# A Fourier mix and a three-way maxout layer on one Trainium2 core: TensorE's order written in the source, the input turned on GpSimd, the fold's output laid out by component, and the opening reordered

## The chip, the cores and the metric

The kernel runs on one core of one Trainium2 chip. The metric is device time in microseconds: the median of several executions. TensorE multiplies (PE in the profile; PEld is its weight load), VectorE is DVE, ScalarE is ACT, GpSimd is POOL, and SP issues the DMAs that store the output. Inputs and outputs are float32 in device memory; the matmuls take bfloat16.

## The reference, cut to what matters

```
def _attn_ref(x):                      # x: (8, 3072, 256)
    X = np.fft.fft(x, axis=1)
    X = np.fft.fft(X, axis=2)
    return X.real
def _moe_ref(x, w1, w2, w3, w_out):    # x: (24576, 256), d_ff = 768
    h = np.maximum(np.maximum(x @ w1, x @ w2), x @ w3)
    return h @ w_out
out = _moe_ref(x=_attn_ref(x).reshape(24576, 256), ...)
```

## The kernel before, in words

The work is done batch by batch (8 batches of 3072 tokens by 256 features). The transform along the sequence is split as 3072 = 24 x 128. The transform along the features is never done by itself: its matrix is multiplied into the weights once, in `prep_first` (gE, gO, gD) and `prep_second` (gw, gwr), so that a batch needs three steps only.

**Step 1, `fnet`, lines 265 to 341.** The input of a batch lies in `x0` as 96 partitions (4 feature groups of 24 rows) by 128 positions by 64 features. For each of the 64 features a matmul of 96 columns (L270) has a 96 x 128 slice of `x0` as its weights and the small matrix `m24blk` as its moving operand. The slice takes every 64th element, so its columns lie 128 bytes apart. Five features fill one PSUM tile `ps`, and ACT copies it into `ub` (L272); the list `DLS` has 13 such groups. DVE then folds feature f with feature 256 - f into sums `zE` and differences `zO` (L280): four operations of 600 elements, eight of 240 and eight of 216, and a few small ones (L289 to L297). `zE` and `zO` have the feature outside and the 24 or 26 components inside. The second stage multiplies by cosine and sine tables, 50 matmuls of up to 128 columns (L318 to L326, and three of one column in L332 to L334); their weights are columns of `zE` or `zO` that lie 48 or 52 bytes apart. ACT writes the result to `tE` and `tO` (L329), and POOL makes reversed copies `tEr` and `tOr` (L339, L340).

**Step 2, units.** A batch has 3 blocks of 512 columns, and a block has 6 units, one for each 128 of the 768 hidden features. In a unit `unit_plus` (L349, L350) runs four matmuls of 512 columns: two into the PSUM tile `pse2` and two into `pse3`. `unit_out` lets ACT write the relu of `pse2` to `stmp` (L363) and DVE take the maximum of `pse3` and `stmp` into `hp` (L364). Then `unit_minus` (L357) adds one more matmul into each of the same two tiles, which makes them the mirrored columns, and `unit_out` runs again, into `hm`. So the added matmul may not start before `hp` has been read out of its tile. Each of `pse2`, `pse3` and `stmp` has two buffers.

**Step 3, the output, `l2_block`.** For each 128 columns of a block 16 matmuls of 256 columns go into a PSUM tile `po` (L367, L369, L372); DVE copies it to `ot` (L392), and SP stores it (L399). These run from a queue, 11 matmuls after each unit, and the rest at the end of a block. A last short piece for one middle row of each batch is `l2_mid`: six little units of 8 columns and 8 matmuls.

**What sets the order.** The source is written in one order, but a scheduler moves the instructions of each engine. Only POOL has its order by hand, in the opening: the 16 DMAs of `x0` for batch 0, with two iotas (`kidx` and `dvec`, L128 and L130) between the fourth and the fifth, then the weights, then `x0` for batch 1. In the opening DVE makes the index tables from `kidx` (L176 to L182), ACT takes their sine into `cos_t` and `sin_t` (L183), and `md` follows from `dvec` (L195 to L205). Engines run their own instructions strictly in order.

Of the kernel before, what the change touches and what calls it, by code (L numbers as in the profile page):

```python
# [9 lines left out]
FP32 = mybir.dt.float32  # L10
# [24 lines left out]
def kernel(  # L35
# [28 lines left out]

    consts = ctx.enter_context(tc.tile_pool(name="consts", bufs=1))
    ps_f = ctx.enter_context(tc.tile_pool(name="ps_f", bufs=2, space=bass.MemoryType.PSUM))
    ps_l1 = ctx.enter_context(tc.tile_pool(name="ps_l1", bufs=2, space=bass.MemoryType.PSUM))
    ps_o = ctx.enter_context(tc.tile_pool(name="ps_o", bufs=2, space=bass.MemoryType.PSUM))
    x0_pool = ctx.enter_context(tc.tile_pool(name="x0", bufs=2))
# [14 lines left out]
    v2_bf = consts.tile([128, 2 * DFF], BF16, tag="v2_bf")  # L84
    v3_bf = consts.tile([128, 2 * DFF], BF16, tag="v3_bf")
# [11 lines left out]
    def load_x0(b, between):  # L97
        x0 = x0_pool.tile([96, 128 * 64], BF16, name="x0", tag="x0")
        xr = x[b].rearrange("(a bb) (g dl) -> g a bb dl", bb=128, g=4)
        x0v = x0.rearrange("p (bb dl) -> p bb dl", dl=64)  # L100
        for ch in range(4):
            if ch in between:
                between[ch]()
            for g in range(4):
                nc.gpsimd.dma_start(  # L105
                    out=x0v[g * 24:(g + 1) * 24, ch * 32:(ch + 1) * 32, :],
                    in_=xr[g, :, ch * 32:(ch + 1) * 32, :])
        return x0
# [17 lines left out]
    def between():  # L126

        nc.gpsimd.iota(kidx, [[1, 13], [24, 128]], base=0, channel_multiplier=0,  # L128
                       allow_small_or_imprecise_dtypes=True)
        nc.gpsimd.iota(dvec, [[1, 64], [64, 2]], base=0, channel_multiplier=0,  # L130
                       allow_small_or_imprecise_dtypes=True)

    with tc.manual_schedule(engines={mybir.EngineType.Pool}):
        x0_tiles = {0: load_x0(0, {1: between})}

# [8 lines left out]
        x0_tiles[1] = load_x0(1, {})  # L144
# [28 lines left out]
    for (dst, shift) in ((cos_t, 768.0), (sin_t, 0.0)):  # L173
        v = gen.tile([128, 13 * 128], FP32, name="v", tag="v", bufs=2)
        q = gen.tile([128, 13 * 128], FP32, name="q", tag="q", bufs=2)
# [14 lines left out]
    for fc in range(2):  # L190
# [10 lines left out]
        vi = gen.tile([128, 256], INT32, name="vi", tag="vi", bufs=2)  # L201
# [14 lines left out]
    for zO in zO_tiles:  # L216
        nc.vector.memset(zO.rearrange("p (c r) -> p c r", r=26)[:, :, 24:26], 0.0)
        nc.vector.memset(zO[:, 0:26], 0.0)

    def prep_first():  # L220

        for jh in range(2):
            cs = slice(jh * 384, (jh + 1) * 384)
            for i, (wv, vv) in enumerate(((w2_bf, v2_bf), (w3_bf, v3_bf))):
                w3d, v3d, w13d = (t.rearrange("p (fc j) -> p fc j", fc=2)[:, :, cs]
                                  for t in (wv, vv, w1_bf))
                tc.keep_in_program_order(
                    nc.vector.tensor_tensor(out=v3d, in0=w3d, in1=w13d, op=ALU.subtract))
                for (half, dst) in ((0, gE[i]), (1, gO[i])):
                    psg = ps_f.tile([128, 512], FP32, name="psg", tag="ps")  # L230
                    for fc in range(2):
# [5 lines left out]
                nc.vector.tensor_scalar(out=gD[i][:, cs], in0=gO[i][:, cs], scalar1=dif,  # L237
                                        scalar2=None, op0=ALU.mult)

    def prep_second():  # L240

        for jp in range(NJC // 2):
# [8 lines left out]
            nc.scalar.copy(out=g1t[:, jp * 512:(jp + 1) * 512], in_=pst)  # L251
        psw = ps_f.tile([128, 512], FP32, name="psw", tag="ps")
        for half in range(2):
            for jc in range(NJC):
# [7 lines left out]
                                op0=ALU.mult)  # L262

    def fnet(b, x0):
        x0r = x0.rearrange("p (bb dl) -> p bb dl", dl=64)
        ub = u_pool.tile([128, 64 * 96], BF16, name="ub", tag="ub")
        for (d0, d1) in DLS:
            ps1 = ps_f.tile([128, 512], FP32, name="ps1", tag="ps")
            for i in range(d1 - d0):
                nc.tensor.matmul(ps1[:, i * 96:(i + 1) * 96], x0r[:, :, d0 + i], m24blk,  # L270
                                 start=True, stop=True)
            nc.scalar.copy(out=ub[:, d0 * 96:d1 * 96], in_=ps1[:, 0:(d1 - d0) * 96])  # L272

# [3 lines left out]
        e = zE.rearrange("p (dl g r) -> p dl g r", g=2, r=24)  # L277
        o = zO.rearrange("p (dl g r) -> p dl g r", g=2, r=26)
        def fold(dst, op, lo, hi, g):
            nc.vector.tensor_tensor(out=dst[:, lo:hi, g, 0:24], in0=u[:, lo:hi, g, :],  # L280
                                    in1=u[:, 64 - lo:64 - hi:-1, 3 - g, :], op=op)

        for ranges in (((20, 45),), ((10, 20), (45, 55)), ((1, 10), (55, 64))):
            for (dst, op) in ((e, ALU.add), (o, ALU.subtract)):
                for (lo, hi) in ranges:
                    for g in range(2):
                        fold(dst, op, lo, hi, g)
                if ranges[0][0] == 1:
                    nc.vector.tensor_tensor(out=dst[:, 0, 1, 0:24], in0=u[:, 0, 1, :],  # L289
                                            in1=u[:, 0, 3, :], op=op)  # L290
                    if dst is e:
                        nc.vector.tensor_copy(e[:, 0, 0, :], u[:, 0, 0, :])

        nc.vector.tensor_scalar(out=o[:, 0, 0, 1:12], in0=u[:, 0, 2, 13:24], scalar1=-1.0,
                                scalar2=None, op0=ALU.mult)
# [130 lines left out]
    for b in range(B):  # L426
        tt = fnet(b, x0_tiles.pop(b))
        if b == 0:
            prep_first()
# [60 lines left out]
```

## Time and profile before

| | us |
|---|---|
| median of 3 runs (lowest to highest) | 500.73 (500.02 to 501.63) |
| the profiled execution's own time | 499.23 |
| its span, from the first to the last instruction | 497.1 |
| PE busy / DVE busy / ACT busy / POOL busy | 453.5 / 320.4 / 260.9 / 140.6 |
| first matmul starts | 27.46 |
| first matmul of the second stage of batch 0 starts | 37.30 |
| first matmul of step 3 starts | 63.69 |

The times in all views count from the start of the span. A matmul's shown duration includes the time in which it drains, so the rate of PE is read from the distance of starts, not from durations. Rows of a view group instructions by line and shape; the mean of one is in ns, and idle time before them stands behind the bar.

### The profile page before, as it was taken

The numbers are of one execution on the slowest core, as the hardware profiler recorded it, in microseconds if no ns is written. First come the engines' busy times: TensorE is split into PE (matmuls) and PEld (weight loads), VectorE is DVE, ScalarE is ACT, GpSimd is POOL, SyncE is SP. The second block draws the span as 40 slices with busy tenths as digits, with TensorE's granted clock in tenths as the row PEclk, the third lists the DMA queues.
The fourth block names the chain that finished last, engine by engine and source line by source line (L and its number), as shares of the span: only waits on it lengthen the run. The fifth ranks groups of instructions, "written<-read, shape, count | busy, mean of one in ns | idle before, by whom it ended". The sixth has DMA issues, their size and how long they took to land.

```text
span 497.1 us, 9195 instructions
## 1 busy us (share of the span) xinstructions
PE 453.5 (91%) x3408; PEld 315.6 (63%) x3408; DVE 320.4 (64%) x662; ACT 260.9 (52%) x472; POOL 140.6 (28%) x160
## 2 busy tenths in 40 slices
PE   0056999999999999999999999999999999999995
PEld 0055447785568657785669666875669566866664
DVE  8834674657676576657666567657675666667663
ACT  1355652575436653575446644665457644765440
POOL 9979800029000750029000840048000100020000
PEclk9999899999999999999999999999999999999998
DMA  8999992219921692219911793119911022102122
GB/s 48 75 164 99 98 32 86 84 44 108 105 86 66 59 133 99 73 44 109 126 65 65 74 123 102 65 46 120 134 64 65 22 65 84 65 22 65 65 84 86
DMA packets 163436, 40.05 MB, mean 81 GB/s; under 512 B 136512, under 2 KB 163392, under 8 KB 163392
## 3 DMA queue, kind: packets, MB, share of 16 engines
q0 software_dynamic: 135536, 14.30, 70.6%
q1 hardware_dynamic: 27856, 25.18, 16.1%
q8 instruction: 26, 0.43, 0.4%
q14 instruction: 18, 0.15, 0.1%
HBM read 28.31 MB, written 25.17 MB: 108 GB/s over the span
## 4 chain that ended last, share of the span: by engine, by line
PE 78%; DVE 3%; ACT 2%; POOL 2%; DMA 1%; issue 1%; DVEq 0%; ACTq 0%
PE po L372 23%; PE pse L349 12%; PE pse L357 11%; PE pse L350 11%; PE ps L270 8%; PE po L367 4%; PE po L369 4%; POOL x L105 2%; PE ps L318 2%; DMA x<-in_x_dram 1%; PE ps L324 1%; PE ps L326 1%; ACT stmp L363 1%; PE ps L321 1%; DVE zE L280 1%
## 5 line engine op out<-in xcount | busy, mean ns | idle before, releaser
L363 ACT ACTIVATE stmp<-pse 128x512 bf16<-128x512 f32 (+1 forms) x294 | 167.7, 588 | 164.3 <-PE pse L350 128.6
L364 DVE TENSOR_TENSOR hp<-pse,stmp 128x512 bf16<-128x512 f32 x144 | 99.1, 690 | 99.1 <-PE pse L357 39.8
L105 POOL DMA_DIRECT2D x<-in_x_dram x128 | 109.5, 863 | 8.1 <-DMA x<-in_x_dram 3.6
L349 PE MATMUL pse<-tE,gE 128*128 128x512 bf16 x288 | 108.8, 379 | 1.7 <-DVE hm L364 0.7
L350 PE MATMUL pse<-tO,gO 128*128 128x512 bf16 x288 | 109.1, 380 | 0.0
L364 DVE TENSOR_TENSOR hm<-pse,stmp 128x512 bf16<-128x512 f32 x144 | 99.0, 687 | 11.8 <-ACT stmp L363 9.3
L357 PE MATMUL pse<-tO,gD 128*128 128x512 bf16 x288 | 94.8, 380 | 1.1 <-ACT stmp L363 0.6
L339 POOL COPY tEr<-tE 128x1536 bf16<-128x1536 bf16 x8 | 11.8, 1471 | 289.1 <-ACT tE L329 289.1
L372 PE MATMUL po<-wout_bf,hp 128*128 128x256 bf16 x576 | 92.6, 272 | 0.0
L372 PE MATMUL po<-wout_bf,hm 128*128 128x256 bf16 x576 | 89.1, 272 | 0.1
L270 PE MATMUL ps<-m24blk,x 96*128 96x96 bf16 x512 | 57.4, 250 | 28.8 <-DMA w_bf<-in_moe_w_dram 27.5
L270 PEld LDWEIGHTS <-x 96*128 96x128 bf16 x512 | 55.9, 199 | 33.1 <-DMA w_bf<-in_moe_w_dram 27.4
L392 DVE COPY ot<-po 128x512 f32<-128x512 f32 x96 | 65.5, 684 | 14.5 <-PE po L372 13.8
L372 PEld LDWEIGHTS <-hm 128*128 128x128 bf16 x576 | 56.1, 99 | 17.3 <-DVE hm L364 0.4
L372 PEld LDWEIGHTS <-hp 128*128 128x128 bf16 x576 | 56.2, 100 | 14.2
L272 ACT CAST ub<-ps 128x480 bf16<-128x480 f32 (+1 forms) x104 | 55.4, 554 | 15.6 <-PE ps L270 13.3
L357 PEld LDWEIGHTS <-gD 128*128 128x128 bf16 x288 | 28.1, 98 | 29.8 <-issue 1.5
L350 PEld LDWEIGHTS <-gO 128*128 128x128 bf16 x300 | 29.4, 98 | 27.1 <-issue 12.2
L349 PEld LDWEIGHTS <-gE 128*128 128x128 bf16 x300 | 29.5, 99 | 21.1 <-issue 2.6
L280 DVE TENSOR_TENSOR zE<-ub 128x240 bf16<-128x240 bf16 (+2 forms) x80 | 20.2, 311 | 33.9 <-ACT ub L272 33.9
L367 PE MATMUL po<-gw,tE 128*128 128x256 bf16 x96 | 26.2, 272 | 0.0
L369 PE MATMUL po<-gwr,tOr 128*128 128x256 bf16 x96 | 26.2, 272 | 0.0
(99 smaller groups left out, 359.5 us busy)
## 6 DMA issues: line engine op xcount, KB each, us to landing
out_dram<-ot SPq DMA_DIRECT2D x176, 128.0 KB, 1.7
x<-in_x_dram POOLq DMA_DIRECT2D x128, 96.0 KB, 6.7
out_dram<-ot SPq DMA_DIRECT2D x24, 64.0 KB, 6.7
w_bf<-in_moe_w_dram POOLq DMA_DIRECT2D x6, 192.0 KB, 6.2
out_dram<-ot SPq DMA_DIRECT2D x8, 63.0 KB
wout_bf<-in_moe_w_out_dram POOLq DMA_DIRECT2D x1, 384.0 KB, 8.6
out_dram<-ot SPq DMA_DIRECT2D x1, 8.0 KB
```

Source lines behind the costliest of these rows:

```text
L105: nc.gpsimd.dma_start(out=x0v[g * 24:(g + 1) * 24, ch * 32:(ch + 1) * 32, :], in_=xr[g, :, ch * 32:(ch + 1) * 32, :])
L270: nc.tensor.matmul(ps1[:, i * 96:(i + 1) * 96], x0r[:, :, d0 + i], m24blk, start=True, stop=True)
L272: nc.scalar.copy(out=ub[:, d0 * 96:d1 * 96], in_=ps1[:, 0:(d1 - d0) * 96])
L349: nc.tensor.matmul(pse[:, 0:n], gE[i][:, js], te, start=True, stop=False)
L350: nc.tensor.matmul(pse[:, 0:n], gO[i][:, js], to, start=False, stop=True)
L357: nc.tensor.matmul(pse, gD[i][:, js], to, start=False, stop=True, skip_group_check=True)
L363: nc.scalar.activation(out=stmp[:, 0:n], in_=pses[0][:, 0:n], func=AX.Relu)
L364: nc.vector.tensor_tensor(out=dst, in0=src3, in1=stmp[:, 0:n], op=ALU.max)
L367: nc.tensor.matmul(po, te, gw[:, 0:256], start=True, stop=False)
L369: nc.tensor.matmul(po, to, wo, start=False, stop=False)
L372: nc.tensor.matmul(po, hcols(jc), wout_bf[:, jc * 256:(jc + 1) * 256], start=False, stop=(jc == NJC - 1))
L392: nc.vector.tensor_copy(out=ot, in_=po)
```

## The change

It has five parts.

1. **PE's and POOL's order is the source's.** The whole main loop stands under a manual schedule for these two engines. Unit u now runs: the added matmul of unit u-1 into `pse2`, the two matmuls into a new `pse2`, the added matmul of unit u-1 into `pse3`, the two into a new `pse3` (L379 to L386). Then come five matmuls of step 3, one step of `fnet` for the next batch, and the other five or six of step 3. `fnet` is now a generator with a step per group of five features or per PSUM tile of the second stage, and a table tells which unit takes which step: units 0 to 12 the 13 groups, units 14 to 17 the second stage. The folds are written right behind groups 4, 8 and 12. DVE and ACT keep the scheduler.
2. **The input is turned on POOL.** From batch 1 on, the DMAs land in four buffers `xs`, and four `tensor_copy` on POOL (L113), 96 partitions by 2048 elements each, write them to `x0` with the 128 positions of one feature side by side. The weights of the first stage (now L298) then have contiguous columns. Batch 0 is still read with a step of 128 bytes.
3. **`zE` and `zO` have the component outside and the feature inside.** The second stage's weights (now L342 to L350) become contiguous. The fold (now L290) runs over features in its inner loop: it writes neighbours and reads `ub` with a step of 192 bytes. It has the same elements as before.
4. **The opening.** All 16 DMAs of batch 0 come ahead of the two iotas. The index table of the sine is made in place in `kidx`, with one buffer each for `v`, `q` and `vi`. Every second PSUM tile of batch 0's first stage is copied by DVE (L301), not by ACT. `prep_first` stands as one piece ahead of the first unit, and takes its differences in place.
5. **The middle row** is two pieces of one PSUM tile each, in units 8 and 10 of the last batch, with one relu and one maximum for all six little units.

The diff, cut to its core:

```
+    FOLDS = {4: ((20, 45),), 8: ((10, 20), (45, 55)), 12: ((1, 10), (55, 64))}
...
+    def fetch_chunk(b, ch):
+        xs = xs_pool.tile([96, 32 * 64], BF16, name="xs", tag="xs")
+        load_chunk(b, ch, xs)
+        return xs
+
+    def turn_chunk(xs, x0, ch):
+
+        nc.gpsimd.tensor_copy(
+            x0.rearrange("p (dl bb) -> p dl bb", bb=128)[:, :, ch * 32:(ch + 1) * 32],
+            xs.rearrange("p (bb dl) -> p dl bb", dl=64))
...
+    with tc.manual_schedule(engines={mybir.EngineType.Pool}):
+        x0_tiles = {0: new_x0(), 1: new_x0()}
+        for ch in range(4):
+            load_chunk(0, ch, x0_tiles[0][:, ch * 2048:(ch + 1) * 2048])
         nc.gpsimd.iota(kidx, [[1, 13], [24, 128]], base=0, channel_multiplier=0,
                        allow_small_or_imprecise_dtypes=True)
...
-        x0_tiles[1] = load_x0(1, {})
+        second = [fetch_chunk(1, ch) for ch in range(4)]
...
         def fold(dst, op, lo, hi, g):
-            nc.vector.tensor_tensor(out=dst[:, lo:hi, g, 0:24], in0=u[:, lo:hi, g, :],
-                                    in1=u[:, 64 - lo:64 - hi:-1, 3 - g, :], op=op)
+            nc.vector.tensor_tensor(
+                out=dst[:, lo:hi, g, 0:24].rearrange("p dl r -> p r dl"),
+                in0=u[:, lo:hi, g, :].rearrange("p dl r -> p r dl"),
+                in1=u[:, 64 - lo:64 - hi:-1, 3 - g, :].rearrange("p dl r -> p r dl"), op=op)
...
+            if b == 0 and i % 2:
+                nc.vector.tensor_copy(ub[:, d0 * 96:d1 * 96], ps1[:, 0:(d1 - d0) * 96])
+            else:
+                nc.scalar.copy(out=ub[:, d0 * 96:d1 * 96], in_=ps1[:, 0:(d1 - d0) * 96])
+            if i in FOLDS:
...
+            yield
...
+    def unit_mm(te, to, jc, last):
...
+        for i in range(2):
+            if last is not None:
+                minus_mm(last, i)
+            pse = ps_l1.tile([128, TOKB], FP32, name=f"pse{i + 2}", tag=f"pse{i + 2}")
+            nc.tensor.matmul(pse, gE[i][:, js], te, start=True, stop=False)
+            nc.tensor.matmul(pse, gO[i][:, js], to, start=False, stop=True)
+            pses.append(pse)
...
+    with tc.manual_schedule(engines={mybir.EngineType.PE, mybir.EngineType.Pool}):
+        tts = {0: []}
+        run(fnet(0, x0_tiles.pop(0), tts[0]), 19)
+        prep_first()
+        for ch in range(4):
+            turn_chunk(second[ch], x0_tiles[1], ch)
...
+                plan = ({6: 2, 7: 2, 8: 2, 9: 2, 10: 2, 11: 2, 12: 1} if b == 0 else
+                        {u: 1 for u in range(13)})
+                plan.update({14: 1, 15: 2, 16: 2, 17: 1})
...
+                n = 11 if jc < 4 else 10
+                l2_some(n // 2)
+                run(steps, plan.get(u, 0))
+                run(extra, int(1 <= u <= 4))
+                l2_some(n - n // 2)
...
+                    if u == 0:
+                        x0_tiles[b + 2] = new_x0()
+                        fetched = [fetch_chunk(b + 2, 0), fetch_chunk(b + 2, 1)]
+                    if u in (4, 8):
+                        turn_chunk(fetched[u // 4 - 1], x0_tiles[b + 2], u // 4 - 1)
+                        fetched.append(fetch_chunk(b + 2, u // 4 + 1))
+                    if u in (11, 14):
+                        turn_chunk(fetched[u // 4], x0_tiles[b + 2], u // 4)
```

How instructions stand now, at three places. First PE in the middle of a batch, one unit, each matmul behind its weight load; before (`gD0` and `gD1` are the weights of the added matmuls; the number behind `pse2` and `pse3` tells the unit's tile):

```order
L349 LDWEIGHTS gE0_98
L349 MATMUL pse2_2055<-tE_1796,gE0_98 128x512
L350 LDWEIGHTS gO0_100
L350 MATMUL pse2_2055<-tO_1797,gO0_100 128x512
L357 LDWEIGHTS gD0_102
L357 MATMUL pse2_2007<-tO_1797,gD0_102 128x512
L349 LDWEIGHTS gE1_99
L349 MATMUL pse3_2056<-tE_1796,gE1_99 128x512
L350 LDWEIGHTS gO1_101
L350 MATMUL pse3_2056<-tO_1797,gO1_101 128x512
L357 LDWEIGHTS gD1_103
L357 MATMUL pse3_2008<-tO_1797,gD1_103 128x512
```

And the same place of the changed kernel:

```order
L386 LDWEIGHTS gD0_103
L386 MATMUL pse2_1939<-tO_1724,gD0_103 128x512
L379 LDWEIGHTS gE0_99
L379 MATMUL pse2_1976<-tE_1723,gE0_99 128x512
L380 LDWEIGHTS gO0_101
L380 MATMUL pse2_1976<-tO_1724,gO0_101 128x512
L386 LDWEIGHTS gD1_104
L386 MATMUL pse3_1943<-tO_1724,gD1_104 128x512
L379 LDWEIGHTS gE1_100
L379 MATMUL pse3_1980<-tE_1723,gE1_100 128x512
L380 LDWEIGHTS gO1_102
L380 MATMUL pse3_1980<-tO_1724,gO1_102 128x512
```

The added matmul into `pse3` of the unit before has moved from the end of the unit to its fourth place, and every unit now has this same order.

Second DVE at the folds in the middle of the run; before:

```order
L364 TENSOR_TENSOR hp<-pse_2367,stmp 128x512
L364 TENSOR_TENSOR hm<-pse_2337,stmp 128x512
L392 COPY ot<-po 128x512
L364 TENSOR_TENSOR hm<-pse_2367,stmp 128x512
L280 TENSOR_TENSOR zE<-ub 128x25x24 x2
L280 TENSOR_TENSOR zO_248<-ub 128x25x24 x2
L392 COPY ot<-po 128x512
L280 TENSOR_TENSOR zE<-ub 128x10x24 x4
L280 TENSOR_TENSOR zO_248<-ub 128x10x24 x4
L280 TENSOR_TENSOR zE<-ub 128x9x24 x4
```

And in the changed kernel, around the first and the second part of the folds:

```order
L393 TENSOR_TENSOR hp<-pse_2777,stmp 128x512
L421 COPY ot<-po 128x512
L290 TENSOR_TENSOR zE<-ub 128x24x25 x2
L290 TENSOR_TENSOR zO_252<-ub 128x24x25 x2
L393 TENSOR_TENSOR hm<-pse_2777,stmp 128x512
```

```order
L393 TENSOR_TENSOR hp<-pse_2932,stmp 128x512
L290 TENSOR_TENSOR zE<-ub 128x24x10 x4
L290 TENSOR_TENSOR zO_252<-ub 128x24x10 x4
L421 COPY ot<-po 128x512
L393 TENSOR_TENSOR hm<-pse_2932,stmp 128x512
L393 TENSOR_TENSOR hp<-pse_2983,stmp 128x512
```

The folds stood behind the last maximum of a batch, with only copies of `ot` between them; now they stand between the `hp` and the `hm` of one unit, and the next unit's `hp` is behind them.

Third DVE in the opening, from the end of the index tables to the first folds of batch 0; before:

```order
L202 CAST vi<-vm 128x256
L205 CAST vm<-vi 128x256
L185 TENSOR_SCALAR nsin_t<-sin_t 128x1664
L203 TENSOR_SCALAR vi<-vi 128x256
L205 CAST vm<-vi 128x256
L280 TENSOR_TENSOR zE<-ub 128x25x24 x2
L280 TENSOR_TENSOR zO_248<-ub 128x25x24 x2
L280 TENSOR_TENSOR zE<-ub 128x10x24 x4
```

And now:

```order
L190 TENSOR_TENSOR kidx<-kidx,q 128x1664
L213 CAST vm<-vi 128x256
L205 TENSOR_SCALAR vm<-dvec,pf 128x128
L301 CAST ub<-ps_266 128x480
L207 TENSOR_SCALAR vm<-pf 128x1
L301 CAST ub<-ps_280 128x480
L193 TENSOR_SCALAR nsin_t<-sin_t 128x1664
L210 CAST vi<-vm 128x256
L301 CAST ub<-ps_298 128x480
L211 TENSOR_SCALAR vi<-vi 128x256
L290 TENSOR_TENSOR zE<-ub 128x24x25
```

DVE's copies of the first stage's PSUM tiles (L301) stand behind the whole chain on `kidx`, and between the rest of the tables and the folds.

## What the change does to the time, predicted blind

> **What bounds the kernel now.** I read the page first, for the share of each engine and the chain that ended last.
>
> ```profile
> span 497.1 us, 9195 instructions
> PE 453.5 (91%) x3408; PEld 315.6 (63%) x3408; DVE 320.4 (64%) x662; ACT 260.9 (52%) x472; POOL 140.6 (28%) x160
> PE 78%; DVE 3%; ACT 2%; POOL 2%; DMA 1%; issue 1%; DVEq 0%; ACTq 0%
> ```
>
> PE is busy for 91% of the span and carries 78% of the last chain. Its idle time is nearly all in the first 37 us. Second, the windows between the POOL copies `tEr` of batches 1 to 7, six whole batches (length, then busy time of PE, PEld, DVE, ACT and POOL, the granted clock, the share of the DMA engines).
>
> ```profile
> 107.86:164.21 56.35, 55.45 (x422) 38.61 (x421) 36.32 (x74) 30.80 (x57) 15.77 (x18) 1.00 0.91 86
> ...
> sum 331.25, PE 329.16 PEld 230.71 DVE 218.64 ACT 186.43 POOL 81.78; mean PE 54.86 PEld 38.45 DVE 36.44 ACT 31.07 POOL 13.63
> ```
>
> A batch takes 331.25 / 6 = 55.2 us, PE works in nearly all of it at full clock, and DVE in 36.4. So a batch costs what PE's stream costs, and that is read from distances of starts in PE's timeline.
>
> ```profile
> 69.52 0.38 PE L350 MATMUL pse<-tO,gO 128*128 128x512 bf16 x1
> 69.74 0.38 PE L357 MATMUL pse<-tO,gD 128*128 128x512 bf16 x1
> ...
> 100.32 0.58 PE L270 MATMUL ps<-m24blk,x 96*128 96x96 bf16 x5
> 100.74 0.27 PE L372 MATMUL po<-wout_bf,hm 128*128 128x256 bf16 x1
> 100.85 0.27 PE L367 MATMUL po<-gw,tE 128*128 128x256 bf16 x1
> ...
> 105.23 0.23 PE L318 MATMUL ps<-cos_t,zE 128*128 128x128 bf16 x1
> 105.30 0.23 PE L321 MATMUL ps<-sin_t,zE 128*128 128x128 bf16 x1
> ```
>
> 512 columns take 0.216 us, 256 take 0.109, five of the first stage 0.42, and 128 columns of the second stage 0.07. Per batch that is 108 x 0.216 = 23.3, 192 x 0.109 = 20.9, 13 x 0.42 = 5.4 and 50 x 0.07 = 3.5: 53.1 us. The other 2.1 us of the 55.2 are waits.
>
> **Contiguous weights.** By the columns that are multiplied, five matmuls of 96 would take 5 x 96/256 x 0.109 = 0.20 us and not 0.42, and 128 columns 0.055 and not 0.07. What differs is the weight load.
>
> ```profile
> L270 PEld LDWEIGHTS <-x 96*128 96x128 bf16 x512 | 55.9, 199 | 33.1 <-DMA w_bf<-in_moe_w_dram 27.4
> L318 PEld LDWEIGHTS <-zE 128*128 128x128 bf16 x104 | 14.6, 162 | 4.8 <-DVE zE L292 4.7
> L372 PEld LDWEIGHTS <-hm 128*128 128x128 bf16 x576 | 56.1, 99 | 17.3 <-DVE hm L364 0.4
> ...
> 483.08 0.17 PE L349 MATMUL pse<-t_mid,gE 128*128 128x8 bf16 x1
> 483.10 0.17 PE L350 MATMUL pse<-t_mid,gO 128*128 128x8 bf16 x1
> ```
>
> A load with a step of 128 bytes takes 199 ns, one of 48 bytes 162, a contiguous one 99. Behind contiguous loads two matmuls of 8 columns start 0.02 us apart, so such a load does not pace anything as wide as 96. I take the column rate: 13 x 0.215 = 2.8 and 50 x 0.055 = 2.7, against 5.4 and 3.5. That is 3.4 us a batch, for seven batches (batch 0 is still read with the step): **-23.8**. If a load paced at its 99 ns, five would take 0.50 and nothing would come of it; the 0.02 excludes that.
>
> **Waits that go.** From the first matmul of step 3 to the end:
>
> ```profile
> 63.69 0.27 PE L367 MATMUL po<-gw,tE 128*128 128x256 bf16 x1
> ...
> 491.45 0.69 DVE L392 COPY ot<-po 128x512 f32<-128x512 f32 x1 [1.05 <-PE po L372]
> ```
>
> are 433.4 us. Work in them: 828 x 0.216 = 178.8 (864 less the first six units), 1536 x 0.109 = 167.4, 7 x 8.9 = 62.3 for the transforms, 3 for the middle row, and 5.7 from 491.4 to the end of the span: 417.2. So 16.2 us are waits: the first block without step 3 beside it, the scheduler's ends of batches, and the middle row's six turns between PE, ACT and DVE. The new order gives each unit of a later block its ten or eleven matmuls of step 3 as cover, so **-16.2**, and +3 for small ones that stay. The middle row in two pieces does 1.5 us less: **-1.5**.
>
> **What the folds cost in their new place.** Here the change gives back. The rows:
>
> ```profile
> L364 DVE TENSOR_TENSOR hp<-pse,stmp 128x512 bf16<-128x512 f32 x144 | 99.1, 690 | 99.1 <-PE pse L357 39.8 <-ACT stmp L363 32.2 <-PE pse L350 26.7
> L392 DVE COPY ot<-po 128x512 f32<-128x512 f32 x96 | 65.5, 684 | 14.5 <-PE po L372 13.8
> ...
> L363 ACT ACTIVATE stmp<-pse 128x512 bf16<-128x512 f32 x288 | 166.6, 597 | 161.6 <-PE pse L350 126.3 <-DVE hp L364 11.4 <-PE pse L357 7.7
> L272 ACT CAST ub<-ps 128x480 bf16<-128x480 f32 x96 | 52.0, 560 | 15.6 <-PE ps L270 13.3
> L280 DVE TENSOR_TENSOR zE<-ub 128x240 bf16<-128x240 bf16 x32 | 6.9, 277 | 2.7 <-ACT ub L272 2.7
> L280 DVE TENSOR_TENSOR zE<-ub 128x600 bf16<-128x600 bf16 x16 | 6.8, 468 | 24.5 <-ACT ub L272 24.5
> L182 DVE TENSOR_TENSOR v<-v,q 128x1664 f32<-128x1664 f32 x2 | 3.7, 1882 | 0.0
> ...
> 50.80 1.29 DVE L364 TENSOR_TENSOR hp<-pse,stmp 128x512 bf16<-128x512 f32 x2
> ```
>
> Two maxima in a row take 1.29, so each costs the queue about 0.61, as does an `ot`. The folds today, on packed bf16, gain an element in (468 - 277) / 360 = 0.53 ns. The two other shapes of the same operation, L364 and L182, need (1882 - 690) / 1152 = 1.03 ns. No row has a fold that reads with a step. Bounds: 0.53 if the step costs nothing, 1.03 and above if it takes the packing away. I take 1.03, since its reads are no longer neighbours; 600 elements are then 0.77 us alone and about 0.70 behind one another, 240 about 0.33, 216 about 0.30. The three bursts are 4 x 0.70 = 2.8, 8 x 0.33 = 2.6 and 8 x 0.30 with six small ones 2.9 us, against 1.6, 1.6 and 2.1 by the lower bound.
>
> The Trainium skill (VectorE: DVE Perf Modes, Mode 2×_1P) asks 16-bit data with a step of one for two elements a cycle, which speaks against this change and for my choice; the 0.53 and the 1.03 are such a pair.
>
> Now one unit, from its start, PE's drain of 0.17 and 0.05 for a wait included. The added matmul into `pse3` ends at 0.86, so `hm` of the unit before runs on DVE from 1.1 and `hp` from 1.7 to 2.4, `ot` to 3.0 where there is one. The group's last matmul ends at 2.1, and ACT's copy to `ub` at 2.9. So the burst begins at 2.9, not earlier. Queued behind it on DVE are `ot` (0.61, not in every unit), the next `hm` (0.61) and `hp` (0.69). PE needs that `hp` at its fourth place two units on, 5.2 to 5.5 + 0.65 = 5.85 to 6.1. First burst: 2.9 + 2.8 + 0.61 + 0.69 + 0.05 = 7.05 against 5.85. Second, with `ot` ahead: 2.9 + 2.6 + 0.61 + 0.61 + 0.69 + 0.05 = 7.46 against 6.1. Third, whose next unit is shorter: 2.9 + 2.9 + 0.61 + 0.61 + 0.69 + 0.05 = 7.76, less about 0.6 where no `ot` falls there, against 5.87. PE stands at the added matmul, with the next two into `pse3` and all of the unit's step 3 queued behind it, for 1.2, 1.4 and 1.3 us, 3.9 a batch: **+27.3** for seven batches. In the kernel before the folds had a stretch of step 3 alone as cover; at the lower bound they wait 0, 0.3 and 0.5 us, +5.6 in all.
>
> **The turn on POOL.**
>
> ```profile
> L339 POOL COPY tEr<-tE 128x1536 bf16<-128x1536 bf16 x8 | 11.8, 1471 | 289.1 <-ACT tE L329 289.1
> ...
> 44.73 3.21 DVE L237 TENSOR_SCALAR gD<-gO,dif 128x384 bf16<-128x384 bf16 x1 [6.00 <-ACT gO L236]
> ...
> 44.94 1.48 POOL L339 COPY tEr<-tE 128x1536 bf16<-128x1536 bf16 x1
> 46.35 1.47 POOL L340 COPY tOr<-tO 128x1536 bf16<-128x1536 bf16 x1
> ```
>
> At this rate 2048 elements are 1.96 us; with reads in steps twice that, 3.9, is the other bound, as with the folds. I take 2.9. Four are 11.6 us a batch beside the 13.6 that POOL works now, and it has 50, and the turn is a batch ahead of its use, so its own time is hidden, and so is its wait for the landing of its four DMAs, behind which the next four issues are queued. For batch 1 it has from about 51, behind `tOr` of batch 0, to 63 us, and PE asks at about 67. The Trainium skill (GPSIMD Engine Reference, Performance pitfalls for Q7 kernels) puts a read whose step is above 8 bytes at half as much again; by that the copy would be an estimated 2.9 us.
>
> But a DVE operation of 384 elements took 3.21 us while these two copies ran, to 47.94, when the second ended: they hold something that DVE needs. A fold that meets a turn would wait for its end. After the 8 DMAs at a batch's start the turns lie near 9, 15, 21 and 25 us, the bursts near 14, 26 and 37; I take a quarter of a turn a batch, 0.7 us, six batches: **+4**.
>
> **The opening.**
>
> ```profile
> 4.89 1.62 POOL L128 IOTA kidx<- 128x1664 f32 x1
> 6.43 0.86 POOL L130 IOTA dvec<- 128x128 f32 x1
> ...
> 8.88 6.57 POOL L105 DMA_DIRECT2D x<-in_x_dram  x1
> ...
> 31.65 0.81 POOL L105 DMA_DIRECT2D x<-in_x_dram  x1 [0.16 <-issue]
> ...
> 9.23 2.07 DVE L176 TENSOR_SCALAR v<-kidx,pidx 128x1664 f32<-128x1664 f32 x2
> 11.23 1.95 DVE L178 TENSOR_SCALAR q<-v 128x1664 f32<-128x1664 f32 x2
> ...
> 27.46 1.09 PE L270 MATMUL ps<-m24blk,x 96*128 96x96 bf16 x10 [27.46 <-DMA w_bf<-in_moe_w_dram]
> ...
> 37.30 0.33 PE L318 MATMUL ps<-cos_t,zE 128*128 128x128 bf16 x1 [1.66 <-DVE zE L292]
> 48.46 0.81 PE L232 MATMUL psg<-v_bf,md 128*128 128x384 bf16 x4 [3.05 <-DVE v_bf L228]
> ```
>
> One DMA's issue stood for 6.57 us while DVE ran the tables; with the iotas behind it this goes, and the input lands about 7 us earlier, near 20 (5.8 of the stall and 2.5 of the iotas, less about 1 as the DMA engines fill). But the tables now start behind 16 issues of 0.81 and both iotas, at 17, not 9.2. Their chain is about 12.4 us, to 29.5 (2.1, twice 1.95 and 3.7 for the eight large ones, 2.7 for the small ones now among them), and DVE's six copies of the first stage stand behind it, with `nsin_t`, the rest of the tables and three bursts: 14 us and 1 of waits. So `zE` is ready near 43 and `zO` near 44.6, not 37.3. Second stage 4 us, `prep_first` 5.5 without the wait of 3.05, six units 36 x 0.216 with the second preparation's 24 matmuls and 1 of waits 11.4: step 3 begins near 65.7, against 63.69: **+2**, between -2 and +8.
>
> **The sum.** 497.1 - 23.8 - 16.2 + 3 - 1.5 + 27.3 + 4 + 2 = 491.9 of span. The profiled execution took 499.23, 2.1 more than its span, so 494.0; the median of the runs is 1.5 above that one, so I forecast **495.5**, 1.0% faster.
>
> **Rivals.** *The folds stay cheap or covered* (faster): at the lower bound 27.3 becomes 5.6, and 474. For it: DVE has 55.2 - 36.4 = 19 us a batch free; against it: the queue behind the burst, and a read without neighbours. Chance 0.18. *Turn and fold collide* (the slower one): DVE stood behind two POOL copies in the row of L237. If a fold does so too, and POOL gets its turn in between two folds of a burst, a whole turn falls into the first and into the second burst. Two of 2.9 us are 5.8 a batch, PE waits as long since the bursts have used up its slack, 6 x 5.8 - 4 = +31, so 526; half of that is 511. It decides from about one whole turn a batch. The Trainium skill (SBUF — State Buffer, Who interferes with whom) has a DVE instruction with two SBUF inputs wait for a GpSimd instruction that reads SBUF, which would be every fold beside a turn; no run so far shows one. L237 speaks for it; the 6.57 us speak against, since there POOL got no gap between DVE's operations. Chance 0.25. *The load is not what paces the small matmuls*, so the contiguous layout does nothing: +23.8, 519; the 0.02 us speaks against. Chance 0.04. My forecast has 0.53, by itself 485 to 505 (the opening's bounds, and bursts of 2 to 4.5 us a batch).
>
> **How the numbers follow.** About 0.3% is what a measurement of this kernel can tell from no change: 499.2 to 502.2. Of the forecast's 0.53 about 0.39 lies below, 0.09 within and 0.05 above; the first rival is faster, the two others slower, but for 0.03 of the collision that ends within. Faster 0.57, same 0.12, slower 0.31. The range of 8 in 10 takes in the first rival and most of the second: 474 to 513.
>
> **What would show it.** Right: first-stage loads near 99 ns from batch 1 on and a group of five in 0.22; folds of 600 near 0.77 us; three waits of about 1.3 us a batch on PE, at the added matmul, released by DVE `hp`; a batch of 54 to 55 us; second stage of batch 0 at 43 to 45. Wrong: folds near 0.47 us or no wait behind them (faster), folds of 3 us beside a turn, or a first-stage matmul of batch 1 that waits for POOL (slower).

## Result: a quarter slower, and the profile after

The changed kernel takes 623.51 us (median of 4 runs, 620.46 to 627.04) against 500.38 before: ratio 1.2463, 95% interval 1.2388 to 1.2539. The forecast was 495.5, with 474 to 513 as its range. The profiled run took 622.65, its span is 620.9.

The page of the changed kernel, span, engines and the clock of its 40 slices:

```profile
span 620.9 us, 9266 instructions
PE 432.1 (70%) x3356; PEld 297.2 (48%) x3408; DVE 461.3 (74%) x663; ACT 250.8 (40%) x461; POOL 243.2 (39%) x188
PEclk9999966898698976999679895899958999999999
```

PE has less work than before (432 against 454 us; the records of 52 of its 3408 matmuls are missing) and stands for 30% of the span; DVE has 141 us more. The windows between the `tEr` copies show where (columns as before: length, busy PE, PEld, DVE, ACT, POOL, clock):

```profile
126.63:202.19 75.56, 53.42 (x411) 36.46 (x417) 57.64 (x74) 30.44 (x56) 31.14 (x22) 0.86 0.49 64
...
501.73:559.14 57.41, 49.92 (x412) 34.77 (x418) 42.68 (x74) 30.49 (x57) 2.92 (x2) 1.00 0.17 56
```

Six batches last from 48.95 to 501.73, 75.5 us each. The last one before the end, in which POOL has nothing to fetch or turn, takes 57.4. Both are longer than the 55.2 before. 6 x 18.1 = 108 us belong to the batches with turns.

The groups by form, busy time and mean ns behind the bar:

```profile
L290 DVE TENSOR_TENSOR zE<-ub 128x600 bf16<-128x600 bf16 x16 | 82.7, 5206 | 0.4 <-ACT ub L303 0.4
L290 DVE TENSOR_TENSOR zO<-ub 128x600 bf16<-128x600 bf16 x16 | 44.3, 2811 | 0.0
L290 DVE TENSOR_TENSOR zE<-ub 128x240 bf16<-128x240 bf16 x32 | 16.1, 566 | 3.1 <-ACT ub L303 3.1
L298 PEld LDWEIGHTS <-x 96*128 96x128 bf16 x512 | 36.9, 114 | 34.1 <-DMA w_bf<-in_moe_w_dram 20.8
L386 PE MATMUL pse<-tO,gD 128*128 128x512 bf16 x288 | 111.3, 387 | 140.8 <-DVE hp L393 140.1
L113 POOL COPY x<-xs 96x2048 bf16<-96x2048 bf16 x28 | 107.3, 3848 | 6.8 <-DMA xs<-in_x_dram 5.4
```

The weight loads fell to 114 ns as expected (batch 0 still has its step). The second stage's matmuls start 0.055 to 0.06 us apart, as expected too; that of batch 0 begins at 43.1, inside the 43 to 45 that were named. Step 3 begins at 68.43 (63.69 before), from PE's timeline:

```profile
68.43 0.27 PE L396 MATMUL po<-gw,tE 128*128 128x256 bf16 x1
...
551.07 0.22 PE L342 MATMUL ps<-cos_t,zE 128*128 128x128 bf16 x1
551.13 0.22 PE L345 MATMUL ps<-sin_t,zE 128*128 128x128 bf16 x1
```

But a fold of 600 into `zE` takes 5.2 us as the mean and one into `zO` 2.8, where 0.77 was forecast, and PE stands 140 us at the added matmul, behind `hp`. POOL's and DVE's timelines around one first burst:

```profile
138.07 3.75 POOL L113 COPY x<-xs 96x2048 bf16<-96x2048 bf16 x1 [0.86 <-DMA xs<-in_x_dram]
141.77 3.22 POOL L102 DMA_DIRECT2D xs<-in_x_dram  x4
144.98 3.63 POOL L113 COPY x<-xs 96x2048 bf16<-96x2048 bf16 x1
148.55 3.23 POOL L102 DMA_DIRECT2D xs<-in_x_dram  x4
151.78 8.13 POOL L113 COPY x<-xs 96x2048 bf16<-96x2048 bf16 x2
```

```profile
139.03 0.68 DVE L393 TENSOR_TENSOR hp<-pse,stmp 128x512 bf16<-128x512 f32 x1
...
142.94 13.48 DVE L290 TENSOR_TENSOR zE<-ub 128x600 bf16<-128x600 bf16 x2
156.34 5.68 DVE L290 TENSOR_TENSOR zO<-ub 128x600 bf16<-128x600 bf16 x2
161.94 0.68 DVE L393 TENSOR_TENSOR hm<-pse,stmp 128x512 bf16<-128x512 f32 x1
```

Four folds last 19.0 us, from 142.94 to 161.94. The two on `zE` end at 149.7 and 156.4, each 1.0 to 1.1 us after a turn (148.6 and 155.4): a fold ran when a turn was done, and the next turn got in before the next fold. A maximum `hp` beside a turn (139.03), which reads PSUM and one SBUF tensor, takes its usual 0.68. In the batch without turns the same burst is this:

```profile
518.03 2.28 DVE L290 TENSOR_TENSOR zE<-ub 128x600 bf16<-128x600 bf16 x2
520.22 2.25 DVE L290 TENSOR_TENSOR zO<-ub 128x600 bf16<-128x600 bf16 x2
522.36 0.70 DVE L393 TENSOR_TENSOR hm<-pse,stmp 128x512 bf16<-128x512 f32 x1
```

4.33 us. So a first burst with turns is 14.7 us longer, the time in which PE does nothing grows by as much (from 7.5 to 22.1 us), and its busy time rises from 49.9 to 53.4 us at a clock of 0.86: 14.7 + 3.5 = 18.2 of the 18.1 us.

### The profile page after: what moved, and what is told of

Read it like the earlier page. It is cut to its first block, busy times and chain, and to the rows that moved or that the text cites. A ratio compares the mean times of both kernels' runs of the same rounds, so it can differ in the third digit from the quotient of the medians.

```text
span 620.9 us, 9266 instructions
## 1 busy us (share of the span) xinstructions
PE 432.1 (70%) x3356; PEld 297.2 (48%) x3408; DVE 461.3 (74%) x663; ACT 250.8 (40%) x461; POOL 243.2 (39%) x188
## 4 chain that ended last, share of the span: by engine, by line
PE 58%; DVE 29%; issue 7%; POOL 2%; ACT 2%; DMA 0%; DVEq 0%; SPq 0%; POOLq 0%
PE po L401 17%; DVE zO L290 11%; PE pse L380 10%; PE pse L386 10%; DVE zE L290 9%; PE pse L379 7%; PE po L396 3%; PE po L398 3%; PE ps L298 3%; DVE hp L393 2%; DVE hm L393 2%; POOL x L102 2%; PE ps L348 1%; DVE ot L421 1%; PE ps L350 1%
## 5 line engine op out<-in xcount | busy, mean ns | idle before, releaser
L392 ACT ACTIVATE stmp<-pse 128x512 bf16<-128x512 f32 x288 | 158.9, 595 | 204.6 <-DVE hm L393 149.2
L386 PE MATMUL pse<-tO,gD 128*128 128x512 bf16 x288 | 111.3, 387 | 140.8 <-DVE hp L393 140.1
L290 DVE TENSOR_TENSOR zE<-ub 128x240 bf16<-128x240 bf16 (+2 forms) x80 | 113.5, 1477 | 6.5 <-ACT ub L303 6.5
L113 POOL COPY x<-xs 96x2048 bf16<-96x2048 bf16 x28 | 107.3, 3848 | 6.8 <-DMA xs<-in_x_dram 5.4
L379 PEld LDWEIGHTS <-gE 128*128 128x128 bf16 x288 | 28.4, 99 | 164.3 <-issue 148.7
L401 PE MATMUL po<-wout_bf,hm 128*128 128x256 bf16 x576 | 95.5, 278 | 0.1
L102 POOL DMA_DIRECT2D xs<-in_x_dram x112 | 91.9, 828 | 2.3 <-DMA xs<-in_x_dram 1.3
L379 PE MATMUL pse<-tE,gE 128*128 128x512 bf16 x238 | 92.5, 389 | 0.0
L421 DVE COPY ot<-po 128x512 f32<-128x512 f32 x96 | 65.9, 686 | 21.7 <-PE po L401 21.4
L290 DVE TENSOR_TENSOR zO<-ub 128x240 bf16<-128x240 bf16 (+2 forms) x80 | 74.8, 994 | 0.0
L298 PE MATMUL ps<-m24blk,x 96*128 96x96 bf16 x512 | 42.2, 221 | 30.7 <-DMA w_bf<-in_moe_w_dram 20.8
L401 PEld LDWEIGHTS <-hm 128*128 128x128 bf16 x576 | 55.2, 100 | 17.2 <-issue 1.1
L298 PEld LDWEIGHTS <-x 96*128 96x128 bf16 x512 | 36.9, 114 | 34.1 <-DMA w_bf<-in_moe_w_dram 20.8
L386 PEld LDWEIGHTS <-gD 128*128 128x128 bf16 x288 | 28.4, 99 | 19.1 <-issue 0.3
```

The lines of the kernel that those rows point to most:

```text
L102: nc.gpsimd.dma_start(out=dst[g * 24:(g + 1) * 24, :].rearrange("p (bb dl) -> p bb dl", dl=64), in_=xr[g, :, ch * 32:(ch + 1) * 32, :])
L113: nc.gpsimd.tensor_copy(x0.rearrange("p (dl bb) -> p dl bb", bb=128)[:, :, ch * 32:(ch + 1) * 32], xs.rearrange("p (bb dl) -> p dl bb", dl ...
L290: nc.vector.tensor_tensor(out=dst[:, lo:hi, g, 0:24].rearrange("p dl r -> p r dl"), in0=u[:, lo:hi, g, :].rearrange("p dl r -> p r dl"), i ...
L298: nc.tensor.matmul(ps1[:, k * 96:(k + 1) * 96], x0r[:, d0 + k, :], m24blk, start=True, stop=True)
L379: nc.tensor.matmul(pse, gE[i][:, js], te, start=True, stop=False)
L386: nc.tensor.matmul(pses[i], gD[i][:, jc * 128:(jc + 1) * 128], to, start=False, stop=True, skip_group_check=True)
```

## The experiments

**Theory A**: a fold, which has two SBUF inputs, stands while POOL reads SBUF in a turn; the turns are the damage and the scattered folds' own length a smaller one. **Rival B**: the scattered access itself makes the folds that slow, with or without turns. Ratios are to the kernel before, with 95% intervals.

**No turn.** Every batch is loaded as batch 0 is, so the first stage's weights have their step again.

```diff
-        second = [fetch_chunk(1, ch) for ch in range(4)]
+        for ch in range(4):
+            load_chunk(1, ch, x0_tiles[1][:, ch * 2048:(ch + 1) * 2048])
...
-            turn_chunk(second[ch], x0_tiles[1], ch)
...
```

> The turn is taken out (every batch loaded straight into x0 as batch 0 is; first stage back to weights with a step), the scattered folds stay. Theory A, POOL holds the folds: in the changed kernel batches with turns last about 75.5 us and the one without 57.4, so without turns each batch is 57.4 plus up to 2.6 for the stepped weight loads: 49 + 7 x 59 + 62 = about 524 us of span (510 to 535), 600-element folds near 1.15 us. Theory B, the scattered access itself makes the folds slow: nothing of that changes, 600-element folds stay at 3 to 5 us, above 600 us.

540.86 us, ratio 1.0823 (1.0761 to 1.0884). A batch, PE's waits, a fold:

```profile
107.71:168.66 60.95, 54.24 (x419) 38.03 (x418) 42.85 (x74) 30.48 (x57) 15.73 (x18) 0.97 0.74 79
```

```profile
PE pse L386 <- DVE hp L393: 45.5, 21, 2.3
```

```profile
L290 DVE TENSOR_TENSOR zE<-ub 128x600 bf16<-128x600 bf16 x16 | 18.4, 1190 | 0.7 <-ACT ub L303 0.6
L290 DVE TENSOR_TENSOR zE<-ub 128x240 bf16<-128x240 bf16 x32 | 16.3, 571 | 3.7 <-ACT ub L303 3.7
```

The folds are at 1.19 us: B falls. But 541 is above A's range: a batch takes 61 us, not 59, since PE is busy for 54.2 us of it and not for 49.9, with the stepped weights again and at a clock of 0.97. Against the blind forecast, the scattered folds alone cost more than it had: 21 waits of 2.2 us.

**Packed folds, turn kept.** Layout and folds of `zE` and `zO` as before the change. (In this run and the next the table `dvec` stayed in the new order of columns and does not match the old one of `zE` and `zO`; the work is the same.)

```diff
-        e = zE.rearrange("p (r g dl) -> p dl g r", g=2, r=24)
+        e = zE.rearrange("p (dl g r) -> p dl g r", g=2, r=24)
...
-                out=dst[:, lo:hi, g, 0:24].rearrange("p dl r -> p r dl"),
+            nc.vector.tensor_tensor(out=dst[:, lo:hi, g, 0:24], in0=u[:, lo:hi, g, :],
...
```

> The folds go back to packed reads and writes (second-stage weights with a step again), the turn stays. Theory A: a packed fold takes 0.47 us alone but stands behind POOL's DMA issues and turns just the same; a batch loses the 5 to 6 us by which the three bursts get shorter and keeps the standing: about 70 us a batch, 575 to 605 in all, folds of 600 with a mean of 2 to 4.5 us. Theory B: folds at 0.47 us, batch of 53 to 55, about 490.

558.14 us (553 to 564), ratio 1.1132 (1.1038 to 1.1226): nearer to A than to B, though below A's range.

```profile
L290 DVE TENSOR_TENSOR zO<-ub 128x600 bf16<-128x600 bf16 x16 | 64.9, 4096 | 0.0
```

```profile
179.42:249.05 69.63, 52.63 (x419) 36.32 (x418) 52.72 (x74) 30.33 (x56) 30.13 (x23) 0.88 0.57 69
...
445.89:496.99 51.10, 50.93 (x419) 35.60 (x418) 35.56 (x74) 30.23 (x56) 2.93 (x3) 1.00 0.19 63
```

The folds into `zO` take 4.1 us as the mean (2.0 into `zE`). In each burst that meets turns two or three of the four packed folds stand, for 1.6 to 10.4 us; the others take their 0.46. So packed folds stand as well: how a fold reads does not matter for that. The batch without turns takes 51.1.

**Neither.** Both edits together: order, place of the folds, opening and middle row are all that is left.

> Both undone: packed folds, no turn; what is left of the change is the order of TensorE, the folds beside the units, and the opening. A and B alike: a batch is PE's 53.1 us and about 1 of waits; 48 + 7 x 54.3 + 61 = about 489 us of span (480 to 498). If it stays at 500 or above, the new order has a cost of its own that neither theory has.

480.37 us, ratio 0.9608 (0.956 to 0.9656).

```profile
95.37:148.77 53.40, 53.33 (x419) 38.23 (x418) 35.69 (x74) 30.17 (x56) 15.74 (x18) 1.00 0.89 90
```

PE works in all of a batch, at full clock. The added matmul, and the start of step 3:

```profile
L384 PE MATMUL pse<-tO,gD 128*128 128x512 bf16 x288 | 108.9, 379 | 1.2 <-ACT stmp L390 0.6
```

```profile
60.85 0.27 PE L394 MATMUL po<-gw,tE 128*128 128x256 bf16 x1
```

Packed folds in the new place cost nothing: 1.2 us of waits there in the whole run.

**Held turns.** The changed kernel with POOL's work at another time. The one-column copy waits for a burst.

```diff
+    def hold(lo):
+        nc.gpsimd.tensor_copy(held[:, 0:1], folded[0][:, lo, 1, 0:1])
...
-                        fetched = [fetch_chunk(b + 2, 0), fetch_chunk(b + 2, 1)]
-                    if u in (4, 8):
...
+                        fetched = [fetch_chunk(b + 2, ch) for ch in range(4)]
+                    if u in (holds := {9: 20, 11: 45} if b == 0 else {5: 20, 9: 45}):
+                        hold(holds[u])
+                        for ch in ((0, 1) if holds[u] == 20 else (2, 3)):
+                            turn_chunk(fetched[ch], x0_tiles[b + 2], ch)
```

> All work of the changed kernel stays; only POOL's time for it moves: all 16 DMA issues at the start of a batch, then a one-column copy out of zO that waits for the first burst of folds, two turns, another such copy behind the second burst, two turns. Theory A: only the end of the DMA issues can still meet the first burst (0 to 2 us a batch); batches of 57.4 to 60 us, 510 to 535 in all. Theory B: as the changed kernel, above 600.

535.29 us, ratio 1.0707 (1.0624 to 1.079), at the upper end of A's range. 88 us go with no work taken away, so it is the meeting and not the turn. POOL, then DVE, at one first burst:

```profile
132.17 1.61 POOL L102 DMA_DIRECT2D xs<-in_x_dram  x2 [0.44 <-issue]
137.08 0.19 POOL L122 COPY held<-zO 128x1 bf16<-128x1 bf16 x1 [3.30 <-DVE zO L298]
137.20 7.41 POOL L113 COPY x<-xs 96x2048 bf16<-96x2048 bf16 x2
```

```profile
132.58 2.28 DVE L298 TENSOR_TENSOR zE<-ub 128x600 bf16<-128x600 bf16 x2
```

Two folds beside DMA issues take 2.28 us, as alone: issues do not stop them.

**Zeros in place of the turn.** Does any work of POOL at SBUF stop a fold, or only its reads? Each turn becomes a one-column copy, for the wait, and a fill; so the batches from the second on compute from zeros.

```diff
-        nc.gpsimd.tensor_copy(
-            x0.rearrange("p (dl bb) -> p dl bb", bb=128)[:, :, ch * 32:(ch + 1) * 32],
-            xs.rearrange("p (bb dl) -> p dl bb", dl=64))
+        nc.gpsimd.tensor_copy(seen, xs[:, 2047:2048])
+        nc.gpsimd.memset(
+            x0.rearrange("p (dl bb) -> p dl bb", bb=128)[:, :, ch * 32:(ch + 1) * 32], 0.0)
```

> The changed kernel with each turn replaced by a one-column copy out of xs (for the same wait) and a fill of the same part of x0 with zeros: GpSimd writes SBUF as before and reads none of it, so the input is left out. Theory R, it is GpSimd's reads of SBUF that shut out a fold with two SBUF inputs: folds of 600 near 1.15 us, batches of 57 to 59, 510 to 535. Theory W, any GpSimd instruction at SBUF does: a fold stands for a whole fill, as long as the fill lasts; if that is near 2 us or more, above 560.

525.17 us, ratio 1.053 (1.0494 to 1.0565). POOL, then DVE:

```profile
123.10 0.59 POOL L113 COPY seen<-xs 96x1 bf16<-96x1 bf16 x1
123.64 1.80 POOL L114 MEMSET x<- 96x2048 bf16 x1
```

```profile
122.47 2.31 DVE L292 TENSOR_TENSOR zE<-ub 128x600 bf16<-128x600 bf16 x2
124.66 2.26 DVE L292 TENSOR_TENSOR zO<-ub 128x600 bf16<-128x600 bf16 x2
```

Folds run through a fill of 1.80 us in 1.1 to 1.2 each: it is POOL's read that shuts them out. The Trainium skill (SBUF — State Buffer, Who interferes with whom) says so of a DVE instruction with two SBUF inputs: it contends with a GpSimd instruction that reads SBUF and not with one that only writes. These runs agree, from both sides. The one-column copy ahead of the fill, which does read SBUF, met a fold that had begun at 122.47: here the fold ran and POOL's copy took 0.59 us, where it takes 0.18 to 0.20 alone.

**Quarters.** Each turn as four copies of 512 elements.

```diff
+        for d0 in range(0, 64, 16):
+            nc.gpsimd.tensor_copy(
+                x0.rearrange("p (dl bb) -> p dl bb", bb=128)[:, d0:d0 + 16, ch * 32:(ch + 1) * 32],
+                xs.rearrange("p (bb dl) -> p dl bb", dl=64)[:, d0:d0 + 16, :])
```

> The changed kernel with each turn cut into four copies of 512 elements, nothing else. Theory A with turns about (a fold gets in after the POOL copy that it met): a fold waits for one piece of about 0.95 us, not 3.6, so the first burst is 4 x 2 us and 2 to 3 of DMA issues instead of 19; a batch near 64 us, 540 to 570. If POOL keeps SBUF for all of its ready work, pieces change nothing: 610 and above.

570.67 us, ratio 1.1449 (1.1397 to 1.1501), at the upper end of the range; a batch is 64.7 us, with 64 expected. DVE, then POOL, at one first burst:

```profile
139.41 6.41 DVE L291 TENSOR_TENSOR zE<-ub 128x600 bf16<-128x600 bf16 x2
145.74 3.94 DVE L291 TENSOR_TENSOR zO<-ub 128x600 bf16<-128x600 bf16 x2
```

```profile
141.80 4.91 POOL L114 COPY x<-xs 96x512 bf16<-96x512 bf16 x4
```

The burst takes 10.3 us and not 19.0, and with 525.2 as the time without meetings (the fills), 98 us of burden become 45. But a fold does not get in behind every piece: the second one, from 141.02 to 145.82, stood through three.

**The turn on ScalarE**, in half pieces, with packed folds.

```diff
-        nc.gpsimd.tensor_copy(
+        nc.scalar.copy(
...
+                    if 8 <= u <= 15:
+                        turn_chunk(fetched[u // 2 - 4], x0_tiles[b + 2], u // 2 - 4, u % 2 * 32)
```

> Packed folds; the turn is done by ScalarE in eight half pieces a batch, beside units 8 to 15, at their place in the program. Theory A: what stops a fold is GpSimd, not the turn: folds stay at 0.47 us beside a turn on ScalarE. ScalarE has 25 us of a batch free and gets 8 pieces of about 1.1 us: batches of 51 to 53 us, 462 to 478 in all. Rival: any engine's turn stops a fold, or the pieces make ScalarE's relu and copies late: above 485.

513.48 us, ratio 1.0282 (1.0249 to 1.0314): a miss in time. A piece, a fold, and two of PE's waits:

```profile
L113 ACT COPY x<-xs 96x1024 bf16<-96x1024 bf16 x56 | 107.9, 1970 | 0.0
```

```profile
L290 DVE TENSOR_TENSOR zE<-ub 128x600 bf16<-128x600 bf16 x16 | 6.8, 461 | 0.4 <-ACT ub L301 0.4
```

```profile
PE pse L384 <- ACT stmp L390: 14.7, 17, 2.9
PE ps L296 <- ACT x L113: 13.5, 5, 5.0
```

The folds stay at 0.46 us, also the four of the burst at 136.63, which ran while a piece did (136.40 to 138.42). So it is POOL and not the turn that stops them. But a piece takes 1.97 us, not 1.1, and PE now waits for ScalarE's relus and for the turned input itself.

**Which side of a scattered fold costs.** Held turns, and the folds run in the other order: packed reads, scattered writes.

```diff
-                out=dst[:, lo:hi, g, 0:24].rearrange("p dl r -> p r dl"),
-                in0=u[:, lo:hi, g, :].rearrange("p dl r -> p r dl"),
+            nc.vector.tensor_tensor(out=dst[:, lo:hi, g, 0:24], in0=u[:, lo:hi, g, :],
```

> As the kernel with held turns (535), but the folds go through their elements in the other order: reads packed, writes scattered, same layout in memory, so the second stage keeps its contiguous weights. If the stepped reads are the price: 600 elements in about 0.5 us and 465 in all. If any step anywhere costs the packing and nothing more: the 1.03 ns an element that the forecast took, 0.77 us, about 490. If crossing lines costs on either side: 1.15 us, about 535.

681.34 us, ratio 1.3647 (1.3607 to 1.3686); all three guesses miss.

```profile
L298 DVE TENSOR_TENSOR zE<-ub 128x600 bf16<-128x600 bf16 x16 | 44.1, 2923 | 0.4 <-ACT ub L309 0.4
...
L298 DVE TENSOR_TENSOR zE<-ub 128x240 bf16<-128x240 bf16 x32 | 37.6, 1462 | 3.1 <-ACT ub L309 3.1
```

(2923 - 1462) / 360 = 4.06 ns an element. Scattered writes are the dearest form; the change had chosen the cheaper one.

**Scattered folds alone in the kernel before**, old place, old order.

```diff
-        e = zE.rearrange("p (dl g r) -> p dl g r", g=2, r=24)
+        e = zE.rearrange("p (r g dl) -> p dl g r", g=2, r=24)
...
+                in0=u[:, lo:hi, g, :].rearrange("p dl r -> p r dl"),
```

> The kernel before with one part of the change: zE and zO in the new layout with scattered folds, in their old place and order, no turn. The three bursts get 6.7 us a batch longer (12.3 against 5.6). Theory P, the place makes them cost: in the old place a stretch of step 3 alone covers part of that; the second stage gets 0.7 us a batch back; 500 to 520. Theory C, the length costs wherever it lies: 500 + 7 x (6.7 - 0.7) = 542 and a few more for the opening.

537.33 us, ratio 1.0763 (1.0739 to 1.0786).

```profile
PE ps L320 <- DVE zE L294: 42.9, 8, 6.2
```

Theory C: the length costs in the old place too. There it is the second stage that waits, eight times, for `zE`.

**Packed folds and held turns**, with `dvec` as before the change.

> Packed folds as before the change, the input turned on GpSimd, but the turns held until the first and the second burst are over. Theory A (a fold stands only where a turn that is ready meets it): with packed folds the one batch without turns took 51.1 us, one without turned input 53.4; held turns should cost nothing: 42.4 + 7 x 51.1 + 62.2 = about 462 us of span, 460 to 472 in all, folds of 600 near 0.47 us. Rival: a turn costs PE or DVE something wherever it lies; then it stays above 480, where the same kernel without turns is.

473.18 us, ratio 0.948 (0.9444 to 0.9515), 1 us above the range. From batch 1 on a batch takes 51.0 us; batch 0 does not:

```profile
42.77:104.62 61.85, 50.93 (x372) 32.78 (x371) 42.17 (x71) 33.89 (x65) 45.26 (x28) 0.94 0.71 56
104.62:155.65 51.03, 50.86 (x419) 35.58 (x418) 35.55 (x74) 30.22 (x56) 30.96 (x25) 1.00 0.88 94
```

**Batch 0's turns behind its third burst**, the same kernel otherwise.

```diff
+                    if b == 0 and u == 13:
+                        hold(63)
+                        for ch in range(4):
+                            turn_chunk(fetched[ch], x0_tiles[2], ch)
```

> The kernel with packed folds and held turns (473.2), with one edit: in batch 0, whose three bursts lie only two units apart, all four turns wait for the third burst. There the second and third burst met held turns (folds of 5.6 and 3.3 us, PE waits of 4.75 and 2.5) and the batch took 61.9 us where the others take 51.0. Theory A: those waits go, batch 0 takes 52 to 55, 464 to 467 in all. Rival: what made batch 0 long is its double steps, not the turns; then 472 again.

467.28 us, ratio 0.9349 (0.9322 to 0.9376): the fastest, 6.5% below the kernel before, at the upper end of the range. POOL and ACT at the end of batch 0:

```profile
82.76 15.23 POOL L113 COPY x<-xs 96x2048 bf16<-96x2048 bf16 x4
97.89 1.51 POOL L371 COPY tEr<-tE 128x1536 bf16<-128x1536 bf16 x1
```

```profile
93.14 0.59 ACT L359 CAST tE<-ps 128x512 bf16<-128x512 f32 x1
```

Here `tEr` (42.49, 97.89) is no measure of the batch, since it stands behind the four turns. From ACT's last `tE` of one batch to the last of the next, 42.43 to 93.73, batch 0 now takes 51.3 us, a little less than expected.

## Why the prediction was wrong

The runs cut the way from 500 to 623.5 into four steps: order, place of the folds and opening 500.3 to 480.4; turned input without meetings to 467.3; scattered folds without meetings to 525.2 (the fills); POOL's reads to 623.5. In the terms of the forecast:

- **Waits that go, middle row, opening**: -16.2 + 3 - 1.5 + 2 = -12.7 forecast, -20.0 measured with packed folds. Right in kind. The opening's +2 was for scattered folds; with them step 3 begins at 68.43 and not at 65.7, +4.7 and inside its bounds. With packed folds it begins at 60.85, 2.8 us earlier than before.
- **Contiguous weights**: five matmuls and the second stage start as forecast (0.06 us from `L342` to `L345`), and a batch falls from 53.4 to 51.0 by the first stage's part, -2.3 where 5.4 - 2.8 = 2.6 stood. Right. That the loads pace the small matmuls holds, and that rival falls.
- **Folds in their new place**: the mechanism, waits at the added matmul for an `hp` behind a burst, three a batch, is right (21 in the run without turns, 21 with fills). The size failed, at the step "I take 1.03, since its reads are no longer neighbours". From the rows of 1190 and 571 in the run without turns, an element costs (1190 - 571) / 360 = 1.72 ns; the first burst took 4.33 us where no turn met it, not 2.8. By the forecast's own working its wait is then 1.2 + 1.5 = 2.7 us; the runs have 2.2 to 2.3 as the mean, not 1.3. Against packed folds the term was 27.3 - 5.6 = +21.7; from 467.3 to 525.2 it was +58, of which the opening is 49.26 - 42.49 = 6.8. A lower bound of 0.53 and a taken value of 1.03 left nothing above, though the text had said "1.03 and above". The lower bound itself was too dear in its place: packed folds wait not 5.6 us but about 1.
- **The turn on POOL**: 3.85 us as the mean (3.6 to 3.8 where it lets no fold by), at the upper bound of 3.9, not 2.9. Hidden by itself, as said.
- **Turn and fold**: the step that failed worst is "I take a quarter of a turn a batch, 0.7 us": +4 against +98. The second rival's mechanism was the right one and was given 0.25 and +31. It priced two turns a batch, one a burst. Its own rule, that POOL gets a turn in between two folds, applies again after each fold: a burst that stands long enough meets the next turn too. Three turns of 3.6 us and the DMA issues between them make 14.7 us, and the lower clock adds 3.5. Even without any meeting the change would have been slower: 525.2 with fills.
- **Folds stay cheap or covered** fell: no scattered fold was cheaper than the taken price, and neither place covers them.

The row of L237 in the profile before, 3.21 us beside two POOL copies, had pointed there. The 6.57 us held against it belonged to a DMA issue, and the held turns show that issues and folds go side by side: a row on another operation was no evidence on the turn. L237 was another operation too, with one tensor as its input; that folds behave like it was shown only by the runs.

## What to carry to other kernels

Two engines with much idle time may still shut each other out. Before a copy is put on GpSimd, look in the trace for a DVE instruction with two SBUF inputs beside a GpSimd copy, and if one stands, give the two a wait that keeps them apart: here one-column copies out of the fold's result, with all DMA issues ahead of them, were worth 88 us. A layout that speeds one engine's reads is paid by whoever writes it: the second stage's contiguous weights, worth 50 x 0.015 = 0.75 us a batch, were bought with folds that made a batch 58.9 us long with fills, where it is 51.2 with packed ones (means of seven batches).

## What the runs showed of the hardware

- **Scattered operands on DVE**: bf16 with two SBUF inputs costs 0.53 ns an element packed, 1.7 with reads 192 bytes apart, 4.1 with writes 256 bytes apart. The Trainium skill (SBUF — State Buffer, Door 1) has a penalty for each access to a new line of 16 bytes; the runs fit that, but no run tells a new line from any other step.
- **A copy with stepped reads**: 2048 elements take POOL 3.75 us, 1.83 ns each, against 1.46 us for 1536 reversed ones, 0.95. The fill with the same writes takes 1.80, so it is the reads. ScalarE needs 1.97 us for 1024.
- **The clock**: after a wait of 17 us PE restarts at half the granted clock (changed kernel: 0.50 from 162 to 166 us, 1.00 from 168), which makes 0.86 over the batch. Waits of 2.2 to 2.6 us can be enough: with held turns batches of 1.00 and 0.97 alternate (57.4 and 59.0 us).
- **Open**: a fold that began at 142.94, 2 us ahead of a turn that was ready behind four DMA issues, stood through the issues as well; beside issues without a turn ready behind them (held turns, fills) folds run freely. Nor is it settled how long a fold stands: mostly for one POOL copy, but in the quarters one fold of a burst stood through three pieces, and with packed folds two stood through two turns (10.4 us). Why was not tried.
